# Linear attention with a gated MLP on one core: batch 0's norm in four blocks of 144 tokens, last keys and values in one load, work dealt to other engines, a new order of all steps

## The chip, the cores and the metric

One core of one Trainium2 chip. The time is the device time of one execution in microseconds; lower is better. The profile is one execution on that core, from its first to its last instruction (the span).

## The reference, cut to what matters

```python
def _attn_ref(q, k, v, g_norm):                     # 8 batches, 8 heads, 576 tokens, 64
    kv = np.einsum('bhsd,bhse->bhde', k, v)
    out = np.einsum('bhsd,bhde->bhse', q, kv)
    rms = np.sqrt(np.mean(out * out, axis=-1, keepdims=True) + 1e-06)
    return out / rms * g_norm
...
def _moe_ref(x, w_in, g_ln, w_sg, b_sg, w_out):     # x: 8 x 576 x 512
    h = gelu_tanh(x @ w_in)                         # 512 -> 1024
    u, v = h[..., :512], h[..., 512:]
    v_n = (v - mean(v)) / np.sqrt(var(v) + 1e-06) * g_ln
    v_s = np.einsum('ts,bsd->btd', w_sg, v_n) + b_sg[None, :, None]
    return x + (u * v_s) @ w_out
```

## The kernel before

Each of the eight batches goes through the same steps, and the steps of several batches are interleaved. A step has a letter, a batch and a number: `K` multiplies keys by values, `o` queries by that product, `s` sums the squares of `o` over a head's columns, `t` makes the reciprocal root. Then `U` and `V` are the two halves of the first MLP product, `S` is the product with `w_sg` over tokens, and `P` the last product, done in seven block products instead of eight.

`K`, `o`, `s` and batch 0's broadcast `M` (L552) run in full f32. `U`, `V`, `S` and `P` (L666, L615, L680 and L683, L741) run in fp32r: every operand is split into a rounded high part and a remainder, and three products are added. So between two such products the other engines evacuate PSUM, apply gelu, the norm or the gate, and make a high part (a cast) and a low part (a subtraction): `z` and `w` for `V`'s result, `H` and `J` for the gated operand, `h` and `W` for sums of gated operands, which `R` (L721) makes. A gated operand is `G` (L693), the product of a gelu'd `u` and the biased `S` (`g`, L688). The weights come as 64-bit words and are turned into f32 by five steps (`A`, `B`, `E`, `L`, `C`), then split (`F`, `I`).

Batches 1 to 7 send the reciprocal roots through DRAM: one DMA out and broadcasting DMAs back (`r`, L539). Batch 0 does not: its eight rows of roots are broadcast by matmuls with a 0/1 matrix, `ext`. Its sums stand as two blocks of 32 rows, one for each half of 288 tokens, in two banks; `rstd` (L494) works on 32 x 288, and each of eight `broadcast` steps is one matmul with 32 rows of `ext`.

What sets the order: nothing is scheduled by the framework (`manual_schedule`). The string `ORDER` names all steps in sequence, and each engine runs its own instructions in that sequence, waiting by semaphore for what they need. A letter behind the name (`v`, `a`, `p`) picks DVE, ACT or POOL where a step has the choice. The table `HOMES` says which buffer or PSUM bank each tile takes. Steps `N` are dummy matmuls on zeros (L270), 69 of them, which fill PE until the first data are there. All loads are issued by SP, in order, over eight DMA semaphores: a DMA may be issued when the one before it on its semaphore has landed. POOL runs the gate `G`, some sums `R`, the reciprocal root of `V`'s variance (L630, L631) and the integer addition of the weights' words (L333).

Of the kernel before, what the change touches and what calls it, by code (L numbers as in the profile page):

```python
# [58 lines left out]
""",  # L59
    h="""  # L60
# [10 lines left out]
""",  # L71
    hv="""
    0 1 2 0 1 2 0 2 0 2 1 2 0 2 1 0 2 1 0 2 0 2 1 0 0 1 2 1 0 1 2 1 0 2 1 0 2 1 0 2
""",
    k="""
    0 1 2 0 1 1 0 2 1 0 0 1 2 2 1 0 1 2 0 1 0 2 1 2 1 1 0 2 1 0 2 1
# [29 lines left out]
    0 1 2 3 0 1 2 3 1 2 0 3 1 2 0 3 1 2 0 3 0 1 2 3 0 3 1 2 0 2 3 1 1 0 2 3
""",
    xo="""
    0 1 2 3 1 2 0 3 1 2 0 3 2 1 0 3 1 3 2 0 3 0 1 2 1 2 0 3 3 1 0 2
""",  # L110
)
WARM = "po1"
# [3 lines left out]
    k01 k02 k04 D21 F21 D23 D02 A02 E02 B02v L02 C02 F02v I02v k00 N899 N898 N897 N896 N895 N894 N893 N892 N891 N890  # L116
    N889 N888 N887 N886 N885 N884 N883 N882 N881 N880 N879 N878 N877 N876 N875 N874 N873 N872 N871 N870 N869 N868 N867
    N866 N865 N864 N863 N862 N861 N860 N859 N858 N857 N856 N855 N854 K00 k03 D00 K01 K02 K03 K04 c00a A00 B00a E00 L00
    C00 F00v I00v q01 N832 N853 N852 N851 N850 N849 N848 N847 N846 N845 N844 o03 e06 o02 e04 q00 o01 e02 o00 q02 o04
    D03 e00 N831 N843 N842 s00 s01 A03 B03v f06a s02 s03 q03 o07 E03 L03 C03 f00v f02v e01 f04a f01v t00 t01 o05 D01  # L120
    A01 e03 f03a o06 E01 k11 s04 s05 e05 s06 e07 s07 t02 t03 B01a L01 D22 t04 t05 M04 x04v t06 t07 M00 D05 N841 N840
    N839 N838 N837 N836 N835 N834 N833 M03 X04v f05a A05 B05a E05 L05 C05 Y04v F03a f07a M07 x07v x03v k12 M02 x02v
    k14 M05 C01 x05v X05a M01 x00v M06 x06v X02a X00a x01v I03v k10 K10 K11 k13 Y00v K12 F01a Y02v Y05v K13 K14 q11
    c10a X06a X07a Y06v X01a q10 o10 e10 e12 D04 q12 e14 A04 I01v U02 f10v e16 q13 f14v o11 B04a e11 e13 e15 D07 e17
    A07 B07a Y01v D20 k22 E04 Y07p L04 s10 s11 s12 f16v C04 F04a X03a f17v s13 t10 E07 f12a f13a t11 t12 U00 t13 t14
    t15 Y03v k21 t16 t17 m0 n02 n03 U01 t18 k20 I04v U04 U07 K20 F20a L07 I21v u02 U06 u04 D06 A06 n01 B06a E06 L06
    D09 A09 C07 B09a u07 I20v C06 F07a U05 u05 D08 f11a r10 F05a I07v U03 F06a I06v u01 k23 k24 D14 K21 I05v A14 E14
# [62 lines left out]
@with_exitstack  # L190
def tile_linear_attn_gmlp(
    ctx: ExitStack,
    tc: tile.TileContext,
    qT: bass.AP,
    kx: bass.AP,
    kl: bass.AP,
    vx: bass.AP,
    vl: bass.AP,
    gn: bass.AP,
    wv: bass.AP,  # L200
    wu: bass.AP,
    wo: bass.AP,
# [489 lines left out]
    def gate(b, n):  # L692
        po.tensor_tensor(u_[b, n], g_[b, n], u_[b, n], op=ALU.mult)  # L693
# [142 lines left out]
```

## Time and profile before

| | |
|---|---|
| three executions, median (lowest to highest) | 495.55 us (493.19 to 495.68) |
| the profiled execution, span | 490.1 us |
| what a timed execution has beside the span | 3.1 to 5.6 us |
| PE / weight loads | 482.1 us (98%) / 440.8 us (90%) |
| DVE / ACT / POOL | 351.3 us (72%) / 179.8 us (37%) / 159.1 us (32%) |
| DMA | 55.36 MB, mean 113 GB/s |

The profiled execution's own time is its span and what lies around it; the page gives the span alone, so the three executions show what lies around. Busy time of PE holds the dummy matmuls too. An engine's idle time counts only where PE waits for it.

### The profile page before, as it was taken

The numbers are of one execution on the slowest core, as the hardware profiler recorded it, in microseconds if no ns is written. First come the engines' busy times: TensorE is split into PE (matmuls) and PEld (weight loads), VectorE is DVE, ScalarE is ACT, GpSimd is POOL, SyncE is SP. The second block draws the span as 40 slices with busy tenths as digits, with TensorE's granted clock in tenths as the row PEclk, the third lists the DMA queues.
The fourth block names the chain that finished last, engine by engine and source line by source line (L and its number), as shares of the span: only waits on it lengthen the run. The fifth ranks groups of instructions, "written<-read, shape, count | busy, mean of one in ns | idle before, by whom it ended". The sixth has DMA issues, their size and how long they took to land.

```text
span 490.1 us, 10060 instructions
## 1 busy us (share of the span) xinstructions
PE 482.1 (98%) x3989; PEld 440.8 (90%) x3989; DVE 351.3 (72%) x809; ACT 179.8 (37%) x442; POOL 159.1 (32%) x204
## 2 busy tenths in 40 slices
PE   6999999999999999999999999999999999999997
PEld 6668889998998999988998998998998899998997
DVE  1698698888777786468765875577767687577576
ACT  1668575155234331142223323335033332123220
POOL 0333142652232323332143113342305232442551
PEclk9999999999999999999999999999999999999999
DMA  8996793054343612064535443300331021100033
GB/s 228 361 353 232 220 277 104 2 157 141 104 142 89 142 43 74 1 192 130 175 75 185 117 104 117 100 1 1 97 104 49 1 62 43 49 1 0 2 122 120
DMA packets 33658, 55.36 MB, mean 113 GB/s; under 512 B 7308, under 2 KB 9228, under 8 KB 33612
## 3 DMA queue, kind: packets, MB, share of 16 engines
q1 hardware_dynamic: 33612, 54.73, 37.1%
q8 instruction: 31, 0.51, 0.4%
q14 instruction: 15, 0.12, 0.1%
HBM read 44.76 MB, written 9.95 MB: 112 GB/s over the span
## 4 chain that ended last, share of the span: by engine, by line
PE 96%; DMA 2%; DVE 0%; ACT 0%; SPq 0%; issue 0%
PE pu L666 21%; PE pg L680 21%; PE pv L615 20%; PE py L741 18%; PE pkv L414 5%; PE pg L683 3%; PE po L439 3%; PE pss L484 2%; DMA kv_first<-in_vx 1%; DMA kv_first<-in_kx 1%; PE psq L468 1%; PE pq L439 1%; PE pb L552 1%; PE warm L270 0%; SPq L405 0%
## 5 line engine op out<-in xcount | busy, mean ns | idle before, releaser
L693 POOL TENSOR_TENSOR u<-gt,u 128x288 f32<-128x288 f32 x64 | 56.3, 890 | 116.3 <-DVE gt L688 113.6
L680 PE MATMUL pg<-wsh,vh 128*128 128x288 f32 x256 | 75.8, 296 | 0.0
L680 PE MATMUL pg<-wso,vh 128*128 128x288 f32 x256 | 75.4, 294 | 0.0
L680 PE MATMUL pg<-wsh,vo 128*128 128x288 f32 x256 | 75.4, 294 | 0.0
L754 DVE SCALAR_TENSOR_TENSOR x<-py,x 128x288 f32<-128x288 f32 x112 | 49.4, 451 | 28.7 <-PE py L741 28.3
L709 DVE TENSOR_TENSOR g<-u,g 128x288 fp32r<-128x288 f32 x112 | 56.2, 517 | 15.7 <-ACT g L230 13.0
L688 DVE SCALAR_TENSOR_TENSOR gt<-pg,glt,b_bc 128x288 f32<-128x288 f32 x64 | 32.3, 512 | 35.2 <-PE pg L683 34.9
L741 PE MATMUL py<-g,woh 128*128 128x288 f32 x256 | 55.9, 295 | 0.0
L230 ACT CAST g<-u 128x288 fp32r<-128x288 f32 x75 | 30.8, 434 | 68.2 <-POOL u L693 52.3
L671 ACT ACTIVATE u<-pu 128x288 f32<-128x288 f32 x64 | 25.7, 411 | 68.3 <-PE pu L666 67.1
L680 PEld LDWEIGHTS pg<-wsh,vh 128*128 128x128 f32 x256 | 48.2, 188 | 0.8 <-DVE gt L688 0.4
L680 PEld LDWEIGHTS pg<-wso,vh 128*128 128x128 f32 x256 | 48.1, 188 | 0.1
L680 PEld LDWEIGHTS pg<-wsh,vo 128*128 128x128 f32 x256 | 48.1, 188 | 0.0
L666 PE MATMUL pu<-xh,wuh 128*128 128x288 f32 x256 | 45.5, 299 | 0.0
L721 POOL TENSOR_TENSOR u<-u 128x288 f32<-128x288 f32 x33 | 29.4, 894 | 49.6 <-DVE g L709 40.9
L666 PE MATMUL pu<-xo,wuh 128*128 128x288 f32 x256 | 44.3, 295 | 0.0
L666 PE MATMUL pu<-xh,wuo 128*128 128x288 f32 x256 | 44.3, 295 | 0.0
L620 ACT ACTIVATE hv<-pv 128x512 f32<-128x512 f32 x32 | 19.0, 598 | 66.5 <-PE pv L615 59.5
L741 PEld LDWEIGHTS py<-g,woh 128*128 128x128 f32 x256 | 42.7, 188 | 0.6 <-issue 0.4
L741 PE MATMUL py<-g,wxh 128*128 128x288 f32 x192 | 41.5, 295 | 0.0
L666 PEld LDWEIGHTS pu<-xh,wuh 128*128 128x128 f32 x256 | 37.6, 188 | 3.7 <-issue 1.9
L741 PE MATMUL py<-g,woo 128*128 128x288 f32 x128 | 37.8, 295 | 0.0
(123 smaller groups left out, 1005.6 us busy)
## 6 DMA issues: line engine op xcount, KB each, us to landing
q<-in_qT SPq DMA_DIRECT2D x32, 288.0 KB, 5.5
out_y<-x SPq DMA_DIRECT2D x28, 288.0 KB, 2.9
bc<-rd SPq DMA_DIRECT2D x28, 256.0 KB, 3.9
k<-in_kx SPq DMA_DIRECT2D x24, 256.0 KB, 4.9
v<-in_vx SPq DMA_DIRECT2D x24, 256.0 KB, 4.8
kv_first<-in_kx SPq DMA_DIRECT2D x8, 256.0 KB, 6.3
kv_first<-in_vx SPq DMA_DIRECT2D x8, 256.0 KB, 5.4
words<-in_wu SPq DMA_DIRECT2D x4, 512.0 KB, 8.4
```

Source lines behind the costliest of these rows:

```text
L230: e.copy(dst, src) if e is ac else e.tensor_copy(dst, src)
L414: nc.tensor.matmul(part["kv", b][64 * r : 64 * r + 64, n * 64 : n * 64 + 64], k_[b, c][:, h], v_[b, c][:, h], start=(c == 0 and n == 0), s ...
L615: nc.tensor.matmul(pv, a[cc], w[:, cc, :], start=(n == 0), stop=(n == 11))
L666: nc.tensor.matmul(pu[:, :HS], w[:, cc, f], a[b, cc][:, t], start=(i == 0), stop=(i == 11))
L671: ac.activation(u_[b, n], part["u", b, n][:, :HS], AF.Gelu_apprx_tanh, scale=W_UP)
L680: nc.tensor.matmul(ps[:, :HS], a[:, d], w[:, c, t], start=(i == 0), stop=False)
L688: ve.scalar_tensor_tensor(g_[b, n], ps[:, :HS], glt[:, dc : dc + 1], b_bc[:, half(n // 4)], op0=ALU.mult, op1=ALU.add)
L693: po.tensor_tensor(u_[b, n], g_[b, n], u_[b, n], op=ALU.mult)
L709: ve.tensor_tensor(lo, src, f32(hi), op=ALU.subtract)
L721: e.tensor_tensor(dst, x, y, op=ALU.subtract)
L741: nc.tensor.matmul(y_[b, bank][c][:, :HS], wo_block(h, blk, e)[:, block(c)], a, start=(start and i == 0), stop=(i == 5), skip_group_check= ...
L754: ve.scalar_tensor_tensor(xs, y_[b, bank][c][:, :HS], W_UP, xs, op0=ALU.mult, op1=ALU.add)
```

## The change

- **Start.** The first loads are two 512 KB blocks of weight words, then batch 0's keys and values. `ext` becomes a tile of its own that POOL sets to zero and four small DMAs from ACT fill.
- **Batch 0's norm.** The sums are four blocks of 144 tokens on 32 rows each, two a bank; the root works on 64 x 144; a broadcast step is two matmuls of 144 columns with 64 rows of `ext`.
- **Last tokens.** The last 64 tokens' keys and values come in one 128 x 512 load a batch instead of two of 64 x 512. `K`'s last matmuls take 64 rows from either half.
- **Engines by step.** `y` (norm of `V`), `w`, `W`, `J`, `G` and `A` get an engine letter. The norm can be an ACT activation with scale and bias; POOL then makes the bias by one more instruction.
- **Order.** `ORDER` and `HOMES` are new throughout.

```diff
     def load_kv(b, c):
-        if c < NC and b < 2:
+        if c == NC:
+            k_[b, c] = T([P, 2, C // 2], F32, "k", 3)
+            sy.dma_start(k_[b, c], kvl[b])
+            return
...
-            nc.tensor.matmul(
-                sums_[0, r][32 * r : 32 * r + 32, :HS],
-                ones[:, ZO - 2 * p : ZO - 2 * p + 32],
-                part["sq", 0, 2 * p + r],
...
+            for j in range(2):
+                at = 64 * r + 32 * j
+                nc.tensor.matmul(
+                    sums_[0, r][at : at + 32, :QS],
+                    ones[:, ZO - 2 * p : ZO - 2 * p + 32],
+                    part["sq", 0, 2 * p + r][:, j * QS : j * QS + QS],
...
     def constants():
+        po.memset(ext, 0.0)
+        for j in range(4):
+            ac.dma_start(ext[32 * j : 32 * j + H, j % 2, :], ex)
...
-    def v_norm(b, c):
+    def v_norm(b, c, e):
         mv, rs = st_[b, c]
-        ve.tensor_scalar(hv_[b, c], hv_[b, c], mv[:, 0:1], rs[:, 0:1], op0=ALU.subtract, op1=ALU.mult)
+        if e is ac:
+            e.activation(hv_[b, c], hv_[b, c], AF.Identity, scale=rs[:, 0:1], bias=mv[:, 2:3])
...
-    def gate(b, n):
-        po.tensor_tensor(u_[b, n], g_[b, n], u_[b, n], op=ALU.mult)
+    def gate(b, n, e):
+        e.tensor_tensor(u_[b, n], g_[b, n], u_[b, n], op=ALU.mult)
...
-    def split_low(b, key, src):
+    def split_low(b, key, src, e):
         hi, lo = gs_[b, key]
-        ve.tensor_tensor(lo, src, f32(hi), op=ALU.subtract)
+        e.tensor_tensor(lo, src, f32(hi), op=ALU.subtract)
...
 ORDER = """
-    k01 k02 k04 D21 F21 D23 D02 A02 E02 B02v L02 C02 F02v I02v k00 N899 N898 N897 N896 N895 N894 N893 N892 N891 N890
+    D02 N899 D00 A00a A02v E02 E00 L00 B02v L02 N898 N897 N896 N895 N894 N893 N892 N891 N890 N889 N888 N887 N886
```

What the table does to the instructions is shown at three places. On SP, the first loads (`kv_first` and the `k`, `v` tiles are batch 0's keys and values, `words` weights, `q` queries). Before:

```order
L405 DMA kv_first<-in_kx 128x512
L405 DMA kv_first<-in_vx 128x512
L405 DMA kv_first<-in_kx 128x512
L405 DMA kv_first<-in_vx 128x512
L405 DMA k<-in_kl 64x512
L405 DMA v<-in_vl 64x512
L295 DMA gnt<-in_gn 128x1
L300 DMA glt<-in_gl 128x4
L287 DMA words<-in_wu 128x2x512
L405 DMA kv_first<-in_kx 128x512
L405 DMA kv_first<-in_vx 128x512
L405 DMA kv_first<-in_kx 128x512
```

Now:

```order
L293 DMA words<-in_wu 128x2x512 x2
L414 DMA kv_first<-in_kx 128x512
L414 DMA kv_first<-in_vx 128x512
L414 DMA kv_first<-in_kx 128x512
L414 DMA kv_first<-in_vx 128x512
L414 DMA kv_first<-in_kx 128x512
L414 DMA kv_first<-in_vx 128x512
L301 DMA gnt<-in_gn 128x1
L414 DMA kv_first<-in_kx 128x512
L414 DMA kv_first<-in_vx 128x512
L407 DMA k<-in_kvl 128x512
L444 DMA q<-in_qT 128x576 x2
```

One load of words has moved ahead of all keys and values and a second with it; the last tokens, two loads in the third pair before, are one load at the end.

On PE, from batch 0's sums of squares (`psq`) through its broadcasts (`pb`) to batch 1's key-value product (`pkv`). Before:

```order
L468 MATMUL psq<-sq,ones 32x288 x4
L439 MATMUL pq<-q,kvf 64x288 x6
L468 MATMUL psq<-sq,ones 32x288 x4
L552 MATMUL pb<-rstd,ext 128x288 x2
L270 MATMUL warm<-zeros 128x256 x9
L552 MATMUL pb<-rstd,ext 128x288 x6
L414 MATMUL pkv<-kv_first 64x64 x32
L414 MATMUL pkv<-v,k 64x64 x8
L439 MATMUL po<-q,kvf 64x288 x8
```

Now:

```order
L483 MATMUL psq<-sq,ones 32x144 x8
L568 MATMUL pb<-rstd,ext 128x144 x6
L427 MATMUL pkv<-kv_first 64x64 x16
L568 MATMUL pb<-rstd,ext 128x144 x6
L427 MATMUL pkv<-kv_first 64x64 x8
L568 MATMUL pb<-rstd,ext 128x144 x2
L427 MATMUL pkv<-kv_first 64x64 x8
L427 MATMUL pkv<-k 64x64 x8
L568 MATMUL pb<-rstd,ext 128x144 x2
L452 MATMUL po<-q,kvf 64x288 x8
```

Batch 1's product now stands between the broadcasts, piece by piece, and no dummy matmuls stand there.

On POOL, its last instructions, all of batch 7 (`u<-gt,u` is the gate, `u<-u` a sum `R`, `g<-u,g` a low part). Before:

```order
L693 TENSOR_TENSOR u<-gt,u 128x288
L721 TENSOR_TENSOR u<-u 128x288
L693 TENSOR_TENSOR u<-gt,u 128x288 x2
L721 TENSOR_TENSOR u<-u 128x288 x2
L693 TENSOR_TENSOR u<-gt,u 128x288 x2
L721 TENSOR_TENSOR u<-u 128x288 x3
L693 TENSOR_TENSOR u<-gt,u 128x288
L721 TENSOR_TENSOR u<-u 128x288
```

Now:

```order
L731 TENSOR_TENSOR g<-u,g 128x288
L743 TENSOR_TENSOR u<-u 128x288
L715 TENSOR_TENSOR u<-gt,u 128x288
L743 TENSOR_TENSOR u<-u 128x288
L731 TENSOR_TENSOR g<-u,g 128x288 x4
L743 TENSOR_TENSOR u<-u 128x288
L731 TENSOR_TENSOR g<-u,g 128x288
L743 TENSOR_TENSOR u<-u 128x288
L731 TENSOR_TENSOR g<-u,g 128x288 x3
```

POOL has taken low parts, on which a `P` waits directly, and given gates to DVE.

## Rows read from the trace of the kernel before

**Rows 1.** The page's first part: busy us (share of the span) xinstructions.
```profile
PE 482.1 (98%) x3989; PEld 440.8 (90%) x3989; DVE 351.3 (72%) x809; ACT 179.8 (37%) x442; POOL 159.1 (32%) x204
```
**Rows 2.** Who PE waited for: us in total, times, longest.
```profile
PE pkv L414 <- DMA kv_first<-in_vx: 2.3, 1, 2.3
...
PE po L439 <- ACT kvf L230: 0.5, 1, 0.5
PE pb L552 <- DVE rstd L508: 0.2, 1, 0.2
```
**Rows 3.** PE in order of time: start, us, line, tile, [idle before <-releaser].
```profile
12.39 2.26 PE L414 MATMUL pkv<-kv_first 128*64 128x64 f32 x64 [2.29 <-DMA kv_first<-in_vx]
...
18.86 2.13 PE L468 MATMUL psq<-sq,ones 128*32 128x288 f32 x8
...
27.42 2.91 PE L552 MATMUL pb<-rstd,ext 32*128 32x288 f32 x12 [0.19 <-DVE rstd L508]
30.26 2.08 PE L414 MATMUL pkv<-kv_first 128*64 128x64 f32 x64
...
33.42 1.20 PE L439 MATMUL po<-q,kvf 64*64 64x288 f32 x16 [0.47 <-ACT kvf L230]
```
**Rows 4.** Each engine's busy time in stretches of the start, with GB/s last.
```profile
0.00:5.00 5.00, 3.20 (x15) 3.20 (x16) 0.71 (x6) 1.49 (x2) 0.19 (x4) 1.00 0.51 137
5.00:9.00 4.00, 4.00 (x26) 4.00 (x26) 0.00 (x0) 0.00 (x0) 0.00 (x0) 1.00 1.06 235
9.00:13.00 4.00, 1.71 (x31) 1.54 (x30) 1.58 (x5) 0.66 (x1) 0.00 (x0) 1.00 1.02 339
13.00:21.00 8.00, 8.00 (x111) 5.46 (x108) 4.25 (x9) 4.13 (x11) 2.59 (x2) 1.00 1.04 389
21.00:29.00 8.00, 7.81 (x42) 4.40 (x43) 7.46 (x17) 6.39 (x15) 1.39 (x2) 1.00 1.07 320
```
**Rows 5.** SP's issues in order of time, and its longest wait for POOL.
```profile
15.90 0.47 SPq L298 DMA_DIRECT2D ext<-in_ex  x1
18.89 0.38 SPq L287 DMA_DIRECT2D words<-in_wv  x1
...
SPq L287 <- POOL w L333: 6.3, 5, 2.2
```
**Rows 6.** ACT in order of time: two steps that waited for words and sums, and a root.
```profile
19.70 0.68 ACT L315 ACTIVATE w<-words 128x512 f32<-128x512 f32 x1 [0.94 <-DMA words<-in_wu]
...
21.34 0.48 ACT L502 ACTIVATE rstd<-psq,eps 32x288 f32<-32x288 f32 x1
...
24.84 0.49 ACT L502 ACTIVATE rstd<-psq,eps 32x288 f32<-32x288 f32 x1 [0.46 <-PE psq L468]
```
**Rows 7.** DVE in order of time: the first step after the first root.
```profile
22.76 0.49 DVE L504 TENSOR_TENSOR rstd<-rstd 32x288 f32<-32x288 f32 x1
```
**Rows 8.** PE in order of time around two full f32 blocks, and PE's first `V`.
```profile
53.13 1.19 PE L615 MATMUL pv<-wvh,xh 128*128 128x512 f32 x4
...
105.37 0.69 PE L666 MATMUL pu<-xh,wuh 128*128 128x288 f32 x4
...
106.95 0.30 PE L741 MATMUL py<-g,woh 128*128 128x288 f32 x1
...
108.63 1.30 PE L414 MATMUL pkv<-v,k 128*64 128x64 f32 x32
109.86 0.80 PE L666 MATMUL pu<-xh,wuh 128*128 128x288 f32 x4
...
111.55 0.29 PE L741 MATMUL py<-g,woh 128*128 128x288 f32 x1
```
**Rows 9.** Instructions by tile: duration in ns, min/median/max.
```profile
L709 DVE TENSOR_TENSOR g<-u,g x112: 424/451/1423, 98.2 to 483.4; 128x288 fp32r<-128x288 f32 x112
...
L693 POOL TENSOR_TENSOR u<-gt,u x64: 797/816/1332, 87.3 to 478.5; 128x288 f32<-128x288 f32 x64
...
L754 DVE SCALAR_TENSOR_TENSOR x<-py,x x112: 424/450/459, 105.7 to 486.9; 128x288 f32<-128x288 f32 x112
```

More of the change, by code (lines that the diff above doesn't have):

```diff
@@ L195, in tile_linear_attn_gmlp @@
     kx: bass.AP,
-    kl: bass.AP,
     vx: bass.AP,
-    vl: bass.AP,
+    kvl: bass.AP,
     gn: bass.AP,
@@ L250, in tile_linear_attn_gmlp @@
     wvs, wos, wss = [], [], []
+    ext = T([P, 2, NP * P], F32, "wsh", nm="ext")
     part = {}
     def constants():
+        po.memset(ext, 0.0)
+        for j in range(4):
+            ac.dma_start(ext[32 * j : 32 * j + H, j % 2, :], ex)
         ve.memset(ones, 0.0)
@@ L295, in load_weight @@
             sy.dma_start(gnt, gn)
-        elif n == 22:
-            part["ext"] = T([64, NP * P], F32, "hv_left", nm="ext")
-            sy.dma_start(part["ext"], ex)
         elif n == 23:
@@ L306, in word_pair, with word_scale @@
         return pair[:, 0], pair[:, 1]
-    def word_scale(n):
+    def word_scale(n, e):
         part["w", n] = T([P, weight(n)[3], 256], I32, *(("hv", 3) if n < 8 else ("h", 28)), nm="w64")
-        ac.mul(f32(part["w", n]), f32(word_pair(n)[1]), W_DOWN)
+        if e is ac:
+            e.mul(f32(part["w", n]), f32(word_pair(n)[1]), W_DOWN)
+        else:
+            e.tensor_scalar(f32(part["w", n]), f32(word_pair(n)[1]), W_DOWN, None, op0=ALU.mult)
     def word_low(n, e):
@@ L398, in load_kv @@
     def load_kv(b, c):
-        if c < NC and b < 2:
+        if c == NC:
+            k_[b, c] = T([P, 2, C // 2], F32, "k", 3)
+            sy.dma_start(k_[b, c], kvl[b])
+            return
+        if b < 2:
             k_[b, c], v_[b, c] = (t[:, c, :] for t in first[b])
         else:
-            n = P if c < NC else LT
-            k_[b, c], v_[b, c] = T([P, C], F32, "k", 3)[:n], T([P, C], F32, "v", 3)[:n]
-        for t, whole, last in ((k_[b, c], kx, kl), (v_[b, c], vx, vl)):
-            sy.dma_start(t, whole[b, :, c, :] if c < NC else last[b])
+            k_[b, c], v_[b, c] = T([P, C], F32, "k", 3), T([P, C], F32, "v", 3)
+        for t, whole in ((k_[b, c], kx), (v_[b, c], vx)):
+            sy.dma_start(t, whole[b, :, c, :])
     def kv(b, n):
@@ L495, in rstd @@
         if b == 0:
-            r, n = slice(32 * (n // 4), 32 * (n // 4) + 32), n % 4
+            r, n = slice(64 * (n // 4), 64 * (n // 4) + 64), n % 4
             if "rstd0" not in part:
-                part["rstd0"] = [T([64, HS], F32, t, nm="rstd") for t in ("xlh", "xlo")]
+                part["rstd0"] = [T([P, QS], F32, t, nm="rstd") for t in ("xlh", "xlo")]
             y, a = (t[r] for t in part["rstd0"])
-            sums = sums_[0, r.start // 32][r, :HS]
+            sums = sums_[0, r.start // 64][r, :QS]
             if n == 0:
@@ L510, in rstd @@
         if n == 0:
-            part["rstd"] = [T([P, QS], F32, t, nm="rstd") for t in ("hv_left", "ry", "bl")]
-        m, y, a = part["rstd"]
+            part["rstd", b] = [T([P, QS], F32, t, nm="rstd") for t in ("hv_left", "ry", "bl")]
+        m, y, a = part["rstd", b]
         if n == 0:
@@ L550, in broadcast @@
         pb = part["pb", n] = PS("pb")
-        r = slice(32 * (n % 2), 32 * (n % 2) + 32)
-        nc.tensor.matmul(
-            pb[:, :HS],
-            part["ext"][r, block(n // 2)],
-            part["rstd0"][0][r],
-            start=True,
-            stop=True,
-            skip_group_check=True,
-            tile_position=(r.start, 0),
-        )
+        r = slice(64 * (n % 2), 64 * (n % 2) + 64)
+        for j in range(2):
+            nc.tensor.matmul(
+                pb[:, j * QS : j * QS + QS],
+                ext[r, j, block(n // 2)],
+                part["rstd0"][0][r],
+                start=True,
+                stop=True,
+                skip_group_check=True,
+                tile_position=(r.start, 0),
+            )
     def scale(b, n, e):
@@ L610, in v @@
         else:
-            xs = [part["xlh"][:, p, :] for p in range(NP)], [part["xlo"][:, p, :] for p in range(NP)]
+            xs = [part["xlh", b // 2][:, p, :] for p in range(NP)], [part["xlo", b // 2][:, p, :] for p in range(NP)]
         n = 0
@@ L640, in v_high @@
             if c % 2 == 0:
-                part["vt"] = [T([P, 2, F], F32R, "vh", 2), T([P, 2, F], F32R, "vo", 2)]
-            vn_[b, c] = [t[:, c % 2] for t in part["vt"]]
+                part["vt", b, c // 2] = [T([P, 2, F], F32R, "vh", 2), T([P, 2, F], F32R, "vo", 2)]
+            vn_[b, c] = [t[:, c % 2] for t in part["vt", b, c // 2]]
             cast(e, vn_[b, c][0], hv_[b, c])
@@ L646, in v_high, with v_low @@
                 s = last_rows(r)[0]
-                part["vl", r] = T([P, F], F32R, "vl%d" % r)
-                cast(e, part["vl", r][s], hv_[b, c][s])
-    def v_low(b, c):
+                part["vl", b // 2, r] = T([P, F], F32R, "vl%d" % r)
+                cast(e, part["vl", b // 2, r][s], hv_[b, c][s])
+    def v_low(b, c, e):
         if c < NC:
             hi, lo = vn_[b, c]
-            ve.tensor_tensor(lo, hv_[b, c], f32(hi), op=ALU.subtract)
+            e.tensor_tensor(lo, hv_[b, c], f32(hi), op=ALU.subtract)
         else:
@@ L656, in v_low @@
                 s, o = last_rows(r)
-                x = part["vl", r]
-                ve.tensor_tensor(x[o], hv_[b, c][s], f32(x)[s], op=ALU.subtract)
+                x = part["vl", b // 2, r]
+                e.tensor_tensor(x[o], hv_[b, c][s], f32(x)[s], op=ALU.subtract)
     def u(b, n):
@@ L682, in s @@
         for w in (w4[1 - r], w4[r]):
-            nc.tensor.matmul(ps[:, :HS], part["vl", r][:, d], w[:, t], start=False, stop=w is w4[r])
+            nc.tensor.matmul(ps[:, :HS], part["vl", b // 2, r][:, d], w[:, t], start=False, stop=w is w4[r])
     def gate_bias(b, n):
@@ L811 @@
     vx, vl = tokens(v)
-    ex = np.zeros((64, NP * P), np.float32)
-    for j in range(2):
-        for h in range(H):
-            ex[32 * j + h, h * 64 : h * 64 + 64] = 1.0
+    kvl = np.stack([kl.reshape(B, LT, 2, 2, P), vl.reshape(B, LT, 2, 2, P)], 2)
+    kvl = con(kvl.transpose(0, 4, 1, 2, 3, 5).reshape(B, P, 2, C // 2))
+    ex = np.zeros((H, NP * P), np.float32)
+    for h in range(H):
+        ex[h, h * 64 : h * 64 + 64] = 1.0
     qT = q.reshape(B, NP, 2, 2, HS, D).transpose(0, 3, 1, 5, 2, 4)
```

224 lines of the change are left out of this document (118 added, 106 removed), and 30 rows, old and new, of tables (h, ps).

## The prediction

> **What bounds the kernel now.** The busy shares come first [rows 1]: PE 98%, no other engine over 72%. A busy PE is not yet a bound PE, since the dummy matmuls count, so the second view is who PE waited for [rows 2]: 4.8 us in all, and nothing after the copy of batch 1's key-value product. The third is PE in order of time [rows 3]: real work begins at 12.39 us, when keys and values have landed; from 27.42 us on PE only works, but for 0.47 us before the `po` of 33.42. So two things set the time: when PE gets to that `po`, and how long the unbroken work after it is (490.1 - 33.4 = 456.7 us). A faster engine beside PE gains nothing after that point; it can only save what it makes PE wait for.
>
> The start is a race of loads. The rates [rows 4] sum to 0.69 MB at 5 us, 1.63 at 9, 2.98 at 13, 6.09 at 21, 8.65 at 29. They are low at first, and drop again to 320 GB/s after 21 us: SP stood from 16.4 to 18.9 us before a load of `wv` words, up to 2.2 us of it for POOL [rows 5], and nothing behind it was issued.
>
> **The change, part by part.**
>
> *Loads.* Through batch 1's last keys and values the queue carries as much as before: 8.66 MB (sizes of the loads, added up), now 8.6. But two 512 KB loads stand first, so more bytes are under way while eight semaphores limit the number of loads, and the `wv` load that waits for POOL comes after three pairs of batch 1's keys and values, when its POOL work is long done. I take 0.69 MB at 5 us as before, the rate of the next stretch (339) from 5 to 9, and 389 from there, the rate of the undisturbed stretch: 2.04 MB at 9, 8.6 at 25.9 us. Before, it was 29.0. Landing comes about 2 us after: the word step at 19.70 waited for its load [rows 6], the queue's first 4.82 MB, which the rates put at 17.7. So batch 1's last keys land at 27.9; their matmuls (a quarter of the 2.26 us of [rows 3]) and the copy (the wait of 0.47) take 1.1 us, so `po` could start at 29.0. The first queries it needs come 0.59 MB later, at 29.4. I take that: 4.0 us before 33.42. If the rates stay as they were, it is 31.0 + 1.1 = 32.1, a gain of 1.3; with 389 from 5 us on, a gain of 4.7. I stay with 4.0, nearer the undisturbed stretch, because the cause of the second dip is removed.
>
> *Batch 0's norm* must be ready by then. Its sums cost 2.13 us a half [rows 3]; with two blocks side by side on different columns I expect about half, 2 us in all. Before, the roots ran on ACT at 21.34 and 24.84 [rows 6], DVE began on the first only at 22.76 [rows 7], and the second's broadcasts started at 27.42. Now the last block of `wu` words, with 5.7 MB ahead of or in it, lands at 20.4; ACT has two steps on it (0.68 each) and a scaling (I take 0.5, as for the root) ahead of the second root: root from 22.3 to 22.8, then three DVE steps (0.49 with twice the columns [rows 7]; I take 0.35), done at 23.8, 3.6 us earlier than before. The broadcasts are 16 short matmuls for 8 long ones, the same columns, and lie between batch 1's pieces while those wait for their loads. So the 2 us of sums go into this chain and are in the 4.0, not beside it. The dummy matmuls after the first keys, 23, become 15; they lie in waits and count nothing either way.
>
> *From there to the first `V`.* Before, it starts at 53.13 [rows 8], 19.7 us after `po`. The same steps stand between, but one key-value piece (1.23) comes later: 29.4 + 19.7 - 1.2 = 47.9. DVE has 51 instructions between the second root and the last low half of `wv`; at 0.45 us, the commonest form's median [rows 9], that is 23 us, to 46.8. The tie costs something: I take 0.2 us, with bounds 0 and 2.
>
> *The new order on PE.* Changing between full f32 and fp32r has a price: a `pu` followed by its like lasts 1.58 us (105.37 to 106.95), a `py` before an f32 block 1.68, a `pu` behind one 1.69 [rows 8]: 0.10 and 0.11 us a change. The sequences of steps have 41 changes before and 57 now. 16 x 0.105 = 1.7 us slower. The key-value block itself lasts 1.23 beside either kind.
>
> *Engines.* Moved to POOL: 51 of 112 gated low parts (0.45 us on DVE, 0.82 for the like on POOL [rows 9]), 12 of 32 low parts of `V`, and one 128 x 1 step for each of 26 norms. Moved off it: 39 gates and sums. POOL gains (51 - 39) x 0.82 + 12 x 1.46 (0.82 scaled to 512 columns) = 27 us and the small steps, an estimate of 200 in all; DVE loses what the low parts and the norms outweigh the gates by, and ACT gains the norms. All stay far under PE's 98%, so on the average this costs nothing; the cover is PE's own work between a product and its use. Where it is thinnest, a result is late: behind batch 7's last `S` products, `P` waits on low parts that stand in a row on POOL. Also a bank is sometimes refilled by the step right behind the one that used it. I take 0.4 us for all such waits, bounds 0 (as before, where none is seen) and 2.5.
>
> *Last keys and values.* Eight loads fewer on SP, the same bytes; `K`'s matmuls keep their number and size. POOL's zeroing of `ext` has no row; at two inputs a 288-column POOL op takes 0.82 us, so 1,024 columns take under 2.9. It gates four small loads and ACT's first steps, which also wait for the second word load; the weights have until 28 us. No cost.
>
> **Sum.** -4.0 + 0.2 + 1.7 + 0.4 = -1.7 us: a span of 488.4 us. The span is 5.45 us under the median of three runs, 495.55; that stays, so 493.9 us.
>
> **Rivals.**
>
> *Full gain (0.22).* The loads come at 389 GB/s from 5 us on, and half of what the first 5 us lack to 235 GB/s is made up (0.25 MB, 0.6 us); no wait is added: 495.55 - 5.3 + 1.7 = 491.9. For it: rows 4 show that rate held for eight microseconds. Against: the first stretches never had it.
>
> *Keys late (0.14), the slower side.* Batch 0's last keys and values now have 3.45 MB ahead of or in them instead of 2.9 (the two word loads, less what stood between before). If their landing, not batch 1's, starts everything, and the way from there to `po` stays 18.8 us (14.65, where the 2.26 us of `pkv` end, to 33.42 [rows 3]), all moves back by 0.55 MB: 1.4 us at 389, 2.3 at 235. With 1.9, 1.7 and 0.4: 499.5 us. It decides if `po` follows the last piece of batch 0's `pkv` by over 14.7 us. Against: that way holds waits behind weight steps on ACT and DVE [rows 6, 7] which the new order puts elsewhere.
>
> *POOL holds DVE up (0.12).* A low part on DVE lasts 0.45 us in the median, but up to 1.42, and POOL's gates stretch from 0.82 to 1.33, while the PSUM additions, with one SBUF input, never pass 0.46 [rows 9]. So two-input operations of these two meet, and there is more to meet now. If one in ten of the 56 `P` steps starts 0.45 us late, that is 2.5 us: 496.4 us. The Trainium skill (SBUF - State Buffer, section "SBUF: two separate sides") states the mechanism: DVE with two SBUF inputs and GpSimd share one port pair as an exclusive lock, held for the whole instruction. It speaks against putting low parts on POOL while DVE takes gates; the rows above agree with it on who is stretched and who is not. The forecast doesn't rest on it, since a stretched operation counts only if PE waits.
>
> **How the numbers follow.** My forecast has 0.52. 0.5% of the time, about what a measurement can tell from no change, is 2.5 us: 493.1 to 498.0 counts as the same. The forecast's own bounds are 495.55 - 4.7 + 1.7 = 492.6 and 495.55 - 1.3 + 2 + 1.7 + 2.5 = 500.5, the latter with every bound at its worst; a third of its chance lies under 493.1 (0.17), the rest within (0.35). Full gain: 0.20 faster. Keys late: 0.12 slower, 0.02 the same. POOL: 0.08 the same, 0.04 slower. Faster 0.37, same 0.47 with what is left, slower 0.16. For 8 in 10 the range reaches from a little under the full gain, 490.5, to 498.5, which leaves out most of the slower rival.
>
> **What would show it.** Right: `po` of batch 1 between 28.7 and 30.5 us; the second root on ACT near 22.5; batch 0's `psq` in two pieces of about 1 us; the first `pv` near 48; 0.1 us more at each of 57 changes; no wait of PE over 0.5 us later. Wrong: `po` after 32 (loads no faster, or keys late); a wait for POOL's `g` or DVE's `vo` or `g` in PE's list; a first `S` that waits for `wso` or the low parts; DMA under 300 GB/s between 9 and 25 us.

## The result, and the profile after

The changed kernel takes 501.24 us in the median of four executions (500.16 to 502.29), the kernel before 495.03 beside it: a ratio of 1.0133 (95% interval 1.0104 to 1.0162), slower by 1.3%. The prediction said 493.9, at most 498.5. The profiled execution took 502.29 us, its span 500.5.

Busy time by engine, after (answers to [rows 1]):

```profile
PE 488.1 (98%) x4021; PEld 443.8 (89%) x4021; DVE 343.2 (69%) x798; ACT 177.0 (35%) x421; POOL 201.6 (40%) x263
```

DVE and ACT have less to do, POOL the 200 us that were estimated, PE 6 us more. Who PE waited for (answers to [rows 2]; total, times, longest):

```profile
PE pkv L427 <- DMA kv_first<-in_vx: 2.0, 2, 1.8
...
PE pkv L427 <- DMA v<-in_vx: 1.3, 2, 0.7
PE pv L631 <- DVE xh L232: 0.9, 1, 0.9
PE pb L568 <- DVE x L581: 0.8, 1, 0.8
```

Before, nothing stood here behind the first `po`; now `pv` and later `pkv` wait. PE in order of time (answers to [rows 3]):

```profile
15.97 0.99 PE L427 MATMUL pkv<-kv_first 128*64 128x64 f32 x16 [1.76 <-DMA kv_first<-in_vx]
16.89 1.12 PE L427 MATMUL pkv<-k 64*64 64x64 f32 x16
18.48 2.20 PE L452 MATMUL pq<-q,kvf 64*64 64x288 f32 x16 [0.47 <-ACT kvf L232]
...
21.76 1.76 PE L483 MATMUL psq<-sq,ones 128*32 128x144 f32 x16
23.45 1.20 PE L452 MATMUL pq<-q,kvf 64*64 64x288 f32 x16
...
34.75 1.20 PE L452 MATMUL po<-q,kvf 64*64 64x288 f32 x16
```

Before, the last piece of batch 0's key-value product was:

```profile
14.58 0.68 PE L414 MATMUL pkv<-v,k 64*64 64x64 f32 x16
```

Now that product ends at 18.0 us (16.89 + 1.12), 2.7 later than before, and the same 16 matmuls of `pq` take 2.20 us at 18.48 and 1.20 at 23.45. The stretches of the start show why (PEclk is the granted clock, the last column GB/s; answers to [rows 4]; the second fence is a second division of the same execution):

```profile
5.00:9.00 4.00, 4.00 (x32) 4.00 (x32) 1.00 (x3) 2.64 (x4) 0.00 (x0) 1.00 0.92 288
9.00:13.00 4.00, 3.83 (x53) 3.36 (x51) 2.30 (x3) 0.91 (x2) 2.97 (x3) 1.00 0.87 201
```

```profile
14.00:16.00 2.00, 0.24 (x4) 0.06 (x4) 0.00 (x0) 0.00 (x0) 1.14 (x1) 1.00 0.98 355
16.00:23.00 7.00, 6.53 (x64) 4.39 (x66) 2.06 (x4) 3.13 (x8) 0.55 (x1) 0.51 1.05 395
23.00:29.00 6.00, 5.38 (x74) 3.60 (x72) 3.58 (x10) 4.65 (x11) 1.49 (x2) 1.00 1.04 374
```

Two things are new. The rate is 201 GB/s from 9 to 13 us, where it was 339. And behind a stretch in which PE was busy 0.24 of 2 us, its clock is at 0.5, that is 1.2 GHz, from 16 to 23 us; in the profiled execution before it was 1.00 all along [rows 4]. The low rate has its cause in SP's issues (answers to [rows 5]):

```profile
4.24 0.33 SPq L414 DMA_DIRECT2D kv_first<-in_vx  x1
7.57 0.33 SPq L414 DMA_DIRECT2D kv_first<-in_kx  x1
...
SPq L414 <- DMA kv_first<-in_kx: 3.3, 2, 3.0
```

For three microseconds SP issued nothing, while it waited for one of its own loads to land: the four small loads of `ext`, issued by ACT, are dealt the same eight semaphores as SP's loads, so one comes round to SP after fewer of its own loads.

From `po` to PE's last matmul it is 462.4 us now, 453.4 before (486.56 + 0.29 - 33.42). Of the 10.4 us by which the span grew, 1.3 lie ahead of `po` and 9.0 between it and PE's last matmul.

### The profile page after: what moved, and what is told of

The parts are those of the page before. It is cut to its first block, busy times and chain, and to the rows that moved or that the text cites. A ratio compares the mean times of both kernels' runs of the same rounds, so it can differ in the third digit from the quotient of the medians.

```text
span 500.5 us, 10159 instructions
## 1 busy us (share of the span) xinstructions
PE 488.1 (98%) x4021; PEld 443.8 (89%) x4021; DVE 343.2 (69%) x798; ACT 177.0 (35%) x421; POOL 201.6 (40%) x263
## 3 DMA queue, kind: packets, MB, share of 16 engines
q1 hardware_dynamic: 33404, 54.60, 37.1%
## 4 chain that ended last, share of the span: by engine, by line
PE 83%; DMA 7%; DVE 6%; ACT 2%; SPq 1%; issue 1%; DVEq 0%
PE pv L631 20%; PE pg L702 18%; PE pu L688 17%; PE py L763 16%; PE pkv L427 4%; PE pg L705 3%; PE po L452 3%; DMA v<-in_vx 2%; DMA bc<-rd 2%; PE pss L499 1%; DMA kv_first<-in_vx 1%; DMA kv_first<-in_kx 1%; PE pq L452 1%; ACT sq L464 1%; DVE x L776 1%
## 5 line engine op out<-in xcount | busy, mean ns | idle before, releaser
L731 POOL TENSOR_TENSOR g<-u,g 128x288 fp32r<-128x288 f32 x51 | 42.1, 836 | 39.6 <-ACT g L232 17.3
L715 POOL TENSOR_TENSOR u<-gt,u 128x288 f32<-128x288 f32 x30 | 26.5, 892 | 60.7 <-DVE gt L710 54.7
L232 ACT CAST g<-u 128x288 fp32r<-128x288 f32 x61 | 25.3, 432 | 60.0 <-DVE u L715 22.1
L339 POOL TENSOR_TENSOR w<-w,words 128x512 int32<-128x512 int32 (+1 forms) x16 | 18.9, 1186 | 51.1 <-DVE w L336 15.6
```

Of the source, the lines that this page charges most:

```text
L232: e.copy(dst, src) if e is ac else e.tensor_copy(dst, src)
L715: e.tensor_tensor(u_[b, n], g_[b, n], u_[b, n], op=ALU.mult)
L731: e.tensor_tensor(lo, src, f32(hi), op=ALU.subtract)
```

## The experiments

Two names are used below: the **chain** is the time from batch 1's first `po` to the end of PE's last matmul, and **held** means that the granted clock shows no fall in the start; where only the mean clock of an execution is known, 0.999 or more counts as held. Ratios are to the kernel before, run beside on the same chip.

**1. Dummies where PE waited (x4_dummies).**

```diff
-    ... N838 N837 K03 ...
+    ... N838 N837 N900 N901 ... N913 K03 ...
```

> Only 14 dummy matmuls (1.6 us) are added in front of batch 0's fourth `pkv` piece, where PE waited 1.76 us. Theory CLOCK (the granted clock of 0.5 from 16.2 to 23.0 us, 1.2 GHz, stretches the chain to `po`): the clock stays 1.0, the fourth piece still starts at about 16.0, the four pieces of `pq` take 1.2 us for 16 instead of 2.2, `po` starts at 32.8 to 33.4, time about 499.5. Rival: the chain waits for ACT and the loads all the same, `po` stays within 0.5 us of 34.75 and the time within 1 us of 501.2.

497.10 us, ratio 1.0074 (1.0050 to 1.0099); the change itself had 1.0133. PE in order of time, the stretch, and what the list of PE's waits has behind `po`:

```profile
13.51 2.17 PE L276 MATMUL warm<-zeros 128*128 128x256 f32 x16
15.84 0.69 PE L427 MATMUL pkv<-kv_first 128*64 128x64 f32 x16 [0.16 <-DMA kv_first<-in_vx]
...
17.62 1.20 PE L452 MATMUL pq<-q,kvf 64*64 64x288 f32 x16 [0.47 <-ACT kvf L232]
...
31.92 1.20 PE L452 MATMUL po<-q,kvf 64*64 64x288 f32 x16
```

```profile
16.00:23.00 7.00, 6.10 (x90) 3.67 (x90) 2.66 (x6) 4.58 (x13) 1.28 (x1) 1.00 1.05 394
```

```profile
PE pss L499 <- ACT sq L464: 0.2, 1, 0.2
...
PE pv L631 <- DVE xh L232: 0.2, 1, 0.2
```

The theory holds, and by more than it said: the fourth piece comes when it came, the clock stays, `po` is 2.8 us earlier, and the median falls by 4.1 us (against the kernel before beside each, the loss falls from 6.2 to 3.6 us). The later waits for `v` and most of those for `xh` are gone as well, and the chain is 458.7. Why they go was not tried apart from this.

**2. The `ext` loads later (x2_ext_late).**

```diff
-        for j in range(4):
-            ac.dma_start(ext[32 * j : 32 * j + H, j % 2, :], ex)
+        elif n == 22:
+            for j in range(4):
+                ac.dma_start(ext[32 * j : 32 * j + H, j % 2, :], ex)
...
-    ... K04 c00a ...
+    ... K04 D22 c00a ...
```

> Only the four ext loads of ACT are moved, from the program's start to just before the copy of batch 0's key-value product. Theory SEMAPHORES (four of the eight DMA semaphores are held by these small loads, so SP stands still from 4.6 to 7.6 us and the rate drops to 141 to 172 GB/s from 9 to 12 us): SP issues the keys without that gap, the rate stays over 250 in every microsecond from 5 to 13, batch 0's fourth `pkv` piece starts before 14.5 instead of 15.97, `po` before 33.2 instead of 34.75, time about 499.5. Rival WORDS (1 MB of words ahead is what makes the keys late): the fourth piece stays within 0.5 us of 15.97 and the time within 1 us of 501.2.

507.18 us, ratio 1.0278 (1.0251 to 1.0305). The fourth piece started at 15.08, between the two forecasts, but ACT's issues and its copy became:

```profile
15.66 6.69 ACTq L301 DMA_DIRECT2D ext<-in_ex  x4
22.39 0.37 ACT L231 COPY kvf<-pkv 128x256 f32<-128x256 f32 x1 [10.26 <-DMA ext<-in_ex]
```

ACT, in order, stood 6.7 us in front of loads whose semaphores SP's large loads held, with the copy behind it, and PE waited 6.4 us. The semaphores are indeed shared; where the small loads stand decides who pays. Without the `ext` loads ahead the product still ended at 16.4 us (15.69 + 0.68), 1.1 later than before: the two word loads ahead have a part in it too.

**3. Keys first (x3_keys_first).**

```diff
-    D02 N899 D00 A00a ... k00 ... k01 k02 ... k03 ... k04 ...
+    k00 k01 k02 k03 k04 D02 N899 D00 A00a ...
```

> Only batch 0's keys and values are loaded ahead of the two word blocks; ext's loads stay at the start. Theory WORDS: batch 0's last `pkv` ends by 14.7 us instead of 18.0, `po` by about 31.5 to 32.5, time about 498.5. Rival SEMAPHORES: the queue still stands still behind the four ext loads, so the last piece ends after 16 and `po` comes after 33.5. Third possibility: the weights are now late, and the first `pu` waits for a `wuh` or `wuo`.

507.75 us, ratio 1.0291 (1.0265 to 1.0318). The last piece of `pkv` ended at 15.6 us, 1.5 earlier than in run 1, with the `ext` loads where they had stood. But ACT in order of time:

```profile
18.79 0.66 ACT L318 ACTIVATE w<-words 128x512 f32<-128x512 f32 x1 [11.17 <-DMA words<-in_wu]
```

Four steps on the words stand ahead of the copy on ACT; `pq` started at 25.23, 9.6 us after the product. The third possibility was nearest: the weights were late, though not for `pu` but on ACT's queue. In this order the words have to come first, and the keys pay for it.

**4. New code, old order (x1_old_order).**

```diff
-ORDER and HOMES of the change
+ORDER and HOMES of before, with G on POOL, y w W J on DVE, A on ACT
```

> The changed code (four blocks of 144 tokens, one load of the last keys and values, ext from ACT) with the order, the buffers and the engines of the kernel before. Theory ORDER (the loss of 6.2 us lies in the new order and the engine letters): the time goes back to 492.5 to 496, with 41 changes between full f32 and fp32r, no wait of PE after the first `po`, and batch 0's sums in two pieces of about 1 us. Rival CODE (the four ext loads or the one load of last tokens cost time wherever they stand): the first `po` stays later than 34 us and the time over 498.

496.27 us, ratio 1.0058 (1.0024 to 1.0092): between the forecasts. PE in order of time:

```profile
15.09 3.37 PE L426 MATMUL pkv<-kv_first 128*64 128x64 f32 x64 [5.03 <-DMA kv_first<-in_vx]
...
22.67 1.17 PE L482 MATMUL psq<-sq,ones 128*32 128x144 f32 x16
...
37.09 1.20 PE L451 MATMUL po<-q,kvf 64*64 64x288 f32 x16 [0.47 <-ACT kvf L231]
```

The chain is 453.5, as before to 0.1 us: what the change costs behind `po` lies in order, buffers and engines, and not in the new code. The start is 3.7 us worse. The keys stand first here and still come 2.7 us later than before, and their matmuls take 3.37 us at the lower clock against 2.26 [rows 3].

**5. The same, `ext` on SP (x5_old_ext_sp).**

```diff
-                ac.dma_start(ext[32 * j : 32 * j + H, j % 2, :], ex)
+                sy.dma_start(ext[32 * j : 32 * j + H, j % 2, :], ex)
...
-    ... B01a L01 t04 ...
+    ... B01a L01 D22 t04 ...
```

> The changed code with the order of before, as in x1_old_order, but the four ext loads are issued by SP where the kernel before had its one ext load, instead of by ACT at the start. Theory SHARED SEMAPHORES (x1's late keys, 15.09 us instead of 12.39, come from the small loads on ACT that stand between SP's loads on the same eight semaphores): `pkv` of batch 0 starts between 12.2 and 12.9, the clock stays at 1.0, `po` of batch 1 starts at or before 33.4, and the time is 492 to 494, no slower than before. Rival CODE: the merged load of the last keys and values, which lands after all the others, still holds `pkv`'s end back to 16 us or later, `po` comes after 35, time 496.

494.61 us, ratio 1.0024 (1.0001 to 1.0048). Batch 0's first piece started at 11.48 and the last ended at 15.2: the four `ext` loads at the start were what had made the keys late in run 4, where SP waited 1.7 and 2.1 us behind its first five loads, and here not. But `pq` then waited, and the clock fell behind that:

```profile
21.35 1.93 PE L452 MATMUL pq<-q,kvf 64*64 64x288 f32 x12 [1.34 <-ACT x L472]
...
37.90 1.20 PE L452 MATMUL po<-q,kvf 64*64 64x288 f32 x16 [0.47 <-ACT kvf L231]
```

```profile
25.00:35.00 10.00, 10.00 (x57) 8.71 (x55) 5.62 (x15) 4.17 (x10) 2.52 (x2) 0.50 0.97 300
```

The twelve executions go from 492.96 to 498.68; the four with a mean clock of 0.993 or less took 496.05 or more. The first half of the sums ends 1.0 us sooner than before (18.83 + 1.17 against 18.86 + 2.13 [rows 3]), and PE stood idle for 1.34 us there: the halved sums leave a gap where the long ones had filled it.

**6. Run 5 with dummies there (x10_old_dummies).**

```diff
-    ... s03 q03 o07 ... s04 e05 s06 ...
+    ... s03 q03 N900 ... N911 o07 ... s04 N912 ... N915 s05 ...
```

> x5_old_ext_sp with 16 dummy matmuls more, where PE waited 1.34 and 0.39 us for ACT in batch 0's `pq` and `psq`. Theory CLOCK (x5's executions of 494.3 to 498.7 us are those in which the granted clock falls): the clock is 1.0 from 8 us on in every execution, none is over 494.5, the median is 492.5 to 493.5. Rival: the dummies stand in the way of `pq` and `psq`, `po` stays after 34 and the median at 494.5 or above.

492.48 us, ratio 0.9959 (0.9942 to 0.9977): faster than both kernels.

```profile
16.04 1.69 PE L453 MATMUL pq<-q,kvf 64*64 64x288 f32 x20
...
19.30 1.68 PE L274 MATMUL warm<-zeros 128*128 128x256 f32 x12
...
32.19 1.20 PE L453 MATMUL po<-q,kvf 64*64 64x288 f32 x16 [0.47 <-ACT kvf L232]
```

Before, that first `pq` was:

```profile
16.69 1.69 PE L439 MATMUL pq<-q,kvf 64*64 64x288 f32 x20
```

`po` comes 1.2 us earlier than before and the chain is 454.0. Of the 1.2 us, 0.65 stand already at `pq`, since the keys came sooner; 0.6 lie in the sums and what follows them. The clock was not held in all: five of the twelve executions have a mean of 0.999 or more, the others 0.995 to 0.998, and one took 494.63.

**7. The kernel before with dummies (x14_before_dummies).**

```diff
-    ... N855 N854 K00 ...
+    ... N855 N854 N900 ... N917 K00 ...
```

> The kernel before with 18 dummy matmuls more (2.1 us) ahead of batch 0's first `pkv`, where PE waits 2.3 us for the loads. Theory CLOCK (in a part of the executions of the kernel before, too, the clock falls in the start, as in x11 and x12, whose start is the same: they have 0.5 from 11.6 to 21.8 and from 30.2 to 33.6 us): fewer executions have a mean clock under 0.998, the median falls by 0.5 to 1.5 us against the kernel before, to about 493. Then x10's 0.4% is the held clock rather than the changed code. Rival: the kernel before holds its clock without them, and the time is the same within 0.3 us; then x10's gain is that of the code.

493.58 us, ratio 0.9992 (0.9975 to 1.0009): no difference shown. In its profiled execution the clock fell behind a stretch with hardly a wait:

```profile
18.00:30.00 12.00, 11.50 (x59) 5.99 (x60) 10.18 (x23) 8.58 (x20) 2.85 (x3) 1.00 1.06 320
30.00:34.00 4.00, 3.92 (x64) 3.50 (x66) 3.69 (x10) 1.62 (x4) 1.71 (x2) 0.58 1.05 388
```

So dummies ahead of the keys alone don't hold it: five of twelve executions have a mean clock of 0.999 or more, against four of the 23 of the kernel before beside it. Of 73 executions of the kernel before, the 12 with a mean clock of 0.999 or more took 493.0 us in the median, the 50 between 494.0, the 11 with 0.993 or less 495.9. The five held ones of run 6 took 491.9, its seven others 492.6. At a like clock run 6 is thus 1.1 to 1.3 us faster, by its code with its dummies; what is left of its 1.7 us is the clock, as far as executions picked by their clock can tell.

**8. Dummies, and `ext` behind ACT's first word steps (x6_dummies_ext).**

```diff
-    ... E02 E00 L00 ... N837 K03 ...
+    ... E02 E00 D22 L00 ... N837 N900 ... N913 K03 ...
```

> The changed kernel with the 14 dummy matmuls of x4_dummies, and the four ext loads moved on ACT from the start to behind its first two word steps (about 7.5 us). Theory SHARED SEMAPHORES: SP issues the third and fourth pair of keys without the stop from 4.6 to 7.6 us, batch 0's last `pkv` piece starts at about 15.7 instead of 16.46, `po` at 31.1 to 31.5 instead of 31.92, time 0.5 to 0.8 us under x4's 497.1. Rival WORDS: the two word loads ahead set the landing of the keys; nothing moves by more than 0.3 us. Against both: ACT may stand behind an ext load that waits for its semaphore, which would make `wuh` and the copy of `pkv` late, and the time as x4 or slower.

497.16 us, ratio 1.0083 (1.0061 to 1.0105), as in run 1: the last piece at 16.53, `po` at 32.41. ACT stood 5 us at the `ext` loads this time, without harm to PE. SP's stop did not go away, it came later; its last loads of batch 0's keys and values were issued at

```profile
7.87 0.33 SPq L415 DMA_DIRECT2D kv_first<-in_kx  x1
9.49 0.33 SPq L415 DMA_DIRECT2D kv_first<-in_vx  x1
11.57 0.33 SPq L408 DMA_DIRECT2D k<-in_kvl  x1
```

with waits of 1.9, 1.3 and 1.7 us before them. So this run moves the stop and gains nothing; it does not show what a start without any would be worth with the words ahead.

**9. The engines back (x7_engines_back).**

```diff
-    ... K03 ... G02v ... J01p ... y12a ... w12p ... W04p ...
+    ... N900 ... N913 K03 ... G02p ... J01v ... y12v ... w12v ... W04v ...
```

> The changed kernel with the 14 dummy matmuls of x4_dummies; gates on POOL, low parts, `V`'s low parts and the norm on DVE, as in the kernel before, the new order kept. Theory ENGINES (moves to POOL and ACT cost PE waits): the short waits at P34, P42, S13 and V20 go, 1 us in all, and the time falls by 0.5 to 1.5 us from x4's 497.1. Rival ORDER: the order was laid out for the new engines, so DVE falls behind in it, new waits for DVE `g` and `vo` appear and the time rises by 1 us or more. Third: within 0.5 us of x4, the engines don't matter beside the 57 changes of format.

512.92 us, ratio 1.0391 (1.0374 to 1.0409), the chain 476.2. What PE waited for:

```profile
PE py L763 <- DVE g L731: 6.5, 9, 1.2
...
PE pg L702 <- DVE vo L675: 1.5, 1, 1.5
```

The new order needs the new engines: with all low parts on DVE they come late, and the time is 15.8 us over run 1's. Which of the five moves matters most was not tried.

**10, 11. The new start with the old order (x9_hybrid, x13_hybrid2).** Up to `po` the changed order with run 1's dummies, then that of before; the second with batch 0's x ahead of the weights' steps.

```diff
-    ... o10 D23 D05 A05a B05a E05 L05 C05 x07v x03v x01v F01a ... e10
+    ... o10 D23 D05 x07v x03v x01v Y02v Y06v X07a X01a F01a e10 ... U02 ... A05a B05a
```

> The changed code; up to batch 1's first `po` the changed order with the 14 dummy matmuls of x4_dummies, from there on the order and the engines of the kernel before (the 15 steps which that order has done by then, 13 of them of weights and of batch 0's x, stand right behind `po`). Theory TWO PARTS (the new start is better once the clock is held, the new order behind it is worse): `po` at 31.7 to 32.3 us as in x4, then 453.4 to 454 us of PE's chain as in the kernel before (458.7 in x4), the span 488.5 to 489.5, the time 490 to 491.5, under the kernel before. Rival DEBT: the 15 steps left over, or weights loaded in another order, make PE wait behind `po` (at the first `V`, or for `wso`), the chain takes 455 or more and the time is 493 or more.

> x9_hybrid with the steps left over put in another order behind batch 1's first `po`: the scaling and splitting of batch 0's x first, the weights' word steps of block 5 only after `U`. Theory DEBT (x9's 2.05 us wait of its first `U` for DVE's x, behind weight steps, and the clock that fell behind it at 35.2 us, are all that kept it from its forecast): no wait of PE over 0.5 us after `po`, `po` at 32 to 32.5, PE's chain from there 453.4 to 454.5 us, time 491 to 492.5. Rival: the word steps now delay `wuh` or the first `V`, a wait of 1 us or more comes up there, and the time stays at 495 or more.

496.20 us, ratio 1.0045 (1.0026 to 1.0064), and 496.06, ratio 1.0041 (1.0023 to 1.0058). `po` came at 32.26 and 32.07 as forecast. Then, of the first and of the second:

```profile
35.51 0.85 PE L688 MATMUL pu<-xh,wuh 128*128 128x288 f32 x2 [2.05 <-DVE x L581]
```

```profile
37.78 0.55 PE L452 MATMUL po<-q,kvf 64*64 64x288 f32 x4 [1.52 <-DVE x L474]
```

The debt moved from one waiting step to the next. In both profiled executions the clock fell behind it, and the chain was 458.0 and 458.3. But the fall is not what keeps the second from its forecast: its five executions with a mean clock of 0.999 or more took 495.9 in the median, all twelve 496.1. The waits named here make 1.5 to 2 us of the 4.5 and 4.9 by which the chains exceed that of before; the rest is open.

**12, 13. What a change of format costs (x11_full_extra, x12_rounded_extra).** In the kernel before, ahead of 32 `U` steps, in full f32 and in fp32r:

```diff
         pu = part["u", b, n] = PS("pu")
+        if 2 <= b < 6:
+            nc.tensor.matmul(pu[:32, :32], ones[:, :32], ones[:, :32], start=True, stop=True, skip_group_check=True)
```

> The kernel before with one more full f32 matmul of 32 rows and 32 columns, of constants, ahead of each of the 32 `U` steps of batches 2 to 5; its result is overwritten by the step's own first product. Theory SWITCH (each change between full f32 and fp32r costs 0.105 us on PE): 32 x 0.21 = 6.7 us, less up to 1.3 where such a step already follows a full block, and 32 times the matmul's own 0.03 to 0.07 us: 6.5 to 9 us slower than the kernel before, and 6 to 7 slower than x12. Rival: the extra 0.1 us is a property of the block products themselves, not of the change, and x11 and x12 differ by under 2 us.

> As x11_full_extra, but the extra matmul is in fp32r, on the high part of x. Theory SWITCH: only its own time is added, 32 x 0.02 to 0.06 = 0.6 to 2 us. Rival: as x11.

505.42 us, ratio 1.0222 (1.0178 to 1.0266; two executions), and 496.69, ratio 1.0050 (1.0023 to 1.0076). The profiled execution of the first also lost some 3 us to the clock in the start (`po` at 36.57), so the price is read from one `U` step of each, from the last products of the step before it to what follows the step:

```profile
200.20 0.69 PE L668 MATMUL pu<-xo,wuh 128*128 128x288 f32 x4
200.81 0.25 PE L665 MATMUL pu<-ones 128*32 128x32 f32 x2
200.99 0.80 PE L668 MATMUL pu<-xh,wuh 128*128 128x288 f32 x4
...
202.69 0.30 PE L682 MATMUL pg<-wsh,vh 128*128 128x288 f32 x1
```

```profile
196.18 0.69 PE L668 MATMUL pu<-xo,wuh 128*128 128x288 f32 x4
196.71 0.18 PE L665 MATMUL pu<-xh 128*32 128x32 f32 x1
196.74 0.77 PE L668 MATMUL pu<-xh,wuh 128*128 128x288 f32 x4
...
198.41 0.29 PE L682 MATMUL pg<-wsh,vh 128*128 128x288 f32 x1
```

2.49 us (200.20 to 202.69) and 2.23 (196.18 to 198.41). Two changes of format, with what the extra matmul itself takes longer in full f32, cost 0.26: at most 0.13 each. The change into full f32, which shows ahead of the extra matmul, is 0.08 of it (200.20 to 200.81, against 196.18 to 196.71). So the theory holds in the main: the chains are 464.3 and 456.8, 7.5 us apart, where it said 6 to 7 and the rival under 2. But the short matmul costs 0.12 with no change at all (196.71 to 198.41 is 1.70, against 1.58 [rows 8]), more than the 0.02 to 0.06 expected of it.

## Why the prediction was wrong, step by step

**What bounds the kernel** was right: the time is set by `po` and by the chain behind it.

**Loads (-4.0): wrong in sign.** The step said that two large loads put more bytes under way. SP stood from 4.6 to 7.6 us, the rate was 201 GB/s from 9 to 13 us instead of 389, batch 0's product ended 2.7 us late, and `po` came 1.3 us late instead of 4.0 early (1.5 early where the clock was held, run 1). The term's error is that it followed batch 1's keys: batch 0's decided, as in the rival Keys late. That rival was nearest in time, in part by luck. The product ended as late as it said where the clock was held (1.9 us in run 1; 1.4 to 2.3), but the way from there to `po`, which it kept, was shorter (18.2 us before, 14.8 held, 16.7 in the changed kernel), and it had no price for the clock. Two things made the keys late in this order: the words ahead (run 3: the product ends 1.5 us sooner than in run 1 with the keys first; run 2: still 1.1 us late without the `ext` loads ahead) and the four `ext` loads, put at no cost, which take semaphores that SP needs (run 2: the fourth piece 0.9 us sooner without them; in the old order, runs 4 and 5, 15.09 against 11.48 for the first `pkv`). The one load of the last tokens is indeed free (run 5: the last piece ends at 15.2).

**"The dummy matmuls ... lie in waits and count nothing either way": the step that failed most.** Held by 14 dummies, the clock gives back 4.1 us of the median; against the kernel before beside it, 3.6 of the 6.2 us of loss are left (run 1). The rows of before showed a clock of 1.00 throughout [rows 4] and so no price for losing it.

**Batch 0's norm.** With the clock held, the sums take 1.17 and 1.42 us (0.44 + 0.98) instead of 2.13 a half, 2.6 in all where 2 was said; the first took 1.76, for the most part at 1.2 GHz, in the changed kernel. The second root ran at 27.5, not 22.5, since all in front of it was late. In run 6 the way from `pq` to `po` is 0.6 us shorter than before (16.15 against 16.73), the most that it shows the new sums to be worth.

**From `po` to the first `V` (+0.2).** 54.60, where 47.9 was said: 5.4 by the late `po`, the rest waits for batch 1's squares (0.6) and batch 2's `v`:

```profile
53.05 1.62 PE L427 MATMUL pkv<-v,k 128*64 128x64 f32 x48 [0.68 <-DMA v<-in_vx]
54.60 1.19 PE L631 MATMUL pv<-wvh,xh 128*128 128x512 f32 x4
```

**The new order on PE (+1.7).** The size was about right: the steps beside a full f32 block cost 0.1 us more in both kernels, at 57 places for 41. The cause holds in the main (runs 12 and 13: at most 0.13 us a change, where 0.105 was said).

**Engines (+0.4; at most 2.5): mis-sized.** With the clock held the chain is 5.2 us longer than before, and run 4 shows that it is order, buffers and engines. The split is an account, not an experiment: 1.7 is the changes; waits that can be named (batch 1's squares 0.6, low parts for `P` 0.6, `K` behind `S` 0.3, `xh` 0.3, `K` to `V` 0.2) make 2.0; the other 1.5 are `V` and `S` steps that last longer, 2.79 and 1.860 us in the median instead of 2.76 and 1.853, and rests. Why a `V` step lasts longer is open. Where the clock fell, the chain has 3.8 us more.

**POOL holds DVE up: seen, but no more than before.** The longest low part on DVE fell from 1,423 ns [rows 9] to 1,059, and the engine letters together are worth 15.8 us in this order (run 9). Added up over DVE's casts, low parts, gates and sums, what goes beyond their medians is 13.4 us, and 13.0 before. In both profiles every one of these operations that lasted over 15% longer than its median (28 now, 26 before) ran beside a POOL instruction, and none that ran alone did. The prediction's reading that two-input operations meet was too narrow: casts, with one input, are stretched too.

```profile
L232 DVE CAST g<-u x51: 276/304/1321, 103.3 to 494.4; 128x288 fp32r<-128x288 f32 x51
```

This agrees with the Trainium skill's rule on the shared port (SBUF — State Buffer, "SBUF: two separate sides"), by which DVE or GpSimd holds a port pair for a whole instruction while the other waits; in which mode the casts ran, no run shows. What it costs is small beside what a second engine takes over.

**Sum and offset.** The span was set 5.45 us under the median. Every execution shown with both has 1.7 to 1.9 between them, not 5.45, so the profiled execution of before took about 491.9: a quick one, whose clock was held, taken for a typical one. With the clock held in both kernels the change is slower by 4.2 us (497.15 against 493.0). The two profiles give 4.9: -1.5 to `po`, +5.2 in the chain, +1.2 behind PE's last matmul.

**What would show it.** The list named a `po` after 32 and a rate under 300 GB/s as signs of error; both came. It did not name the granted clock. (With 389 GB/s from 5 us on, the prediction's own rates give a gain of 4.6, not 4.7; nothing hangs on it.)

## What to carry to other kernels

Before calling dummy work or a shortened step free, ask what keeps TensorE's clock up through the next wait, and look at the granted clock of each stretch in more than one execution. Count every load of every engine against the semaphores that they share, and read the start by the first product, not by the last load. An order and the engines that it was laid out for go together: undoing one alone costs more than either.

## What was not expected of the hardware

The clock fell in quite different company: in the changed kernel behind a wait of 1.76 us, in run 7 behind twelve microseconds in which PE was busy 96% (11.50 of 12.00), while a wait of 2.29 us in the profiled execution before [rows 3] left it at 1.00. The same program has it in some executions and not in others; what decides is not shown by these runs. A 32-column fp32r matmul ahead of a 288-column step costs 0.12 us (1.70 against 1.58), though the next matmul starts 0.03 us behind it (196.71 to 196.74).
